# A three-stage attention and expert kernel: each step of its blocks cut into one-engine pieces, and the pieces issued in one fixed order

## The chip, the core and the metric

The kernel runs on one core of one Trainium2 chip. TensorE (PE) multiplies matrices and transposes, VectorE (DVE) and GpSimd (POOL) work element by element, ScalarE (ACT) applies exp and copies, and SyncE (SP) starts the transfers. The time is the device time of one execution in microseconds (us). Before the change the median of three runs is 252.41 us (251.99 to 254.53).

## The reference

x is (2, 11456, 128) in float32. Three layers follow one another:

```python
def mab(q, kv):                       # attention, scale = 1/sqrt(128)
    s = scale * (q @ kv.transpose(0, 2, 1))
    s = s - s.max(-1, keepdims=True)
    a = np.exp(s)
    a /= a.sum(-1, keepdims=True) + 1e-09
    return a @ kv
h = mab(I, x)                         # 32 inducing points look at all tokens of a batch
x1 = mab(x, h).reshape(22912, 128)    # every token looks at the 32 rows of h

logits = x1 @ phi                     # 32 slots, softmax over all 22912 tokens
d = np.exp(logits - logits.max(0)); d /= d.sum(0) + 1e-09
slots = (d.T @ x1).reshape(8, 4, 128) # 8 experts with 4 slots each
slot_out[e] = np.maximum(slots[e] @ w1[e], 0) @ w2[e]
c = np.exp(logits - logits.max(1)); c /= c.sum(1) + 1e-09
x2 = c @ slot_out                     # a softmax over the slots of each token

# third layer: cosine logits to 8 expert vectors, argmax, out = gate * (relu(x2 @ w1[e]) @ w2[e])
```

## The kernel before, in words

The tokens are cut into 12 blocks, six for each batch: five of 4 quads (a quad is 4 tiles of 128 tokens) and one of 2 quads. A thirteenth, "sp", holds the tokens left over. Each block goes through two phases.

**Phase 1** (lines 168 to 222) makes h of each batch. `p1_transpose` turns the tokens on PE (tile xTps) and copies them to xT, but only for the blocks in `ON_PE`; for the others xT comes ready by a transfer. `p1_scores` makes the scores s against the inducing points, their extreme mb, the running extreme mn, and on ACT e = exp and corr, the factor for what was summed before. `p1_etrans` transposes e (eTps), and `p1_h` makes the weighted sums (hps) and adds them to hacc, times corr. When the sixth block of a batch is done, `finish_h` makes hT from hacc (tiles fps, den, hT; lines 276 to 319) and from hT what phase 2 needs: BD, hst and a few bounds. A block's phase-2 scores read hT of its batch, so none can start before hT exists.

**Phase 2** (lines 321 to 459): `p2_scores` (s against hT), `p2_soft` (transposes s2T, maximum mx, difference sh, exp), `p2_a2q` (transposes a2q), `p2_logits` (lps; the row sums sm and their reciprocal; the weights a on POOL; logits lT; column maximum ml). `p2_max` and `p2_max2` keep a running maximum over the tokens: ml is transposed (mps), reduced (m32b), spread (dg, mps) and joined with the old one (mnew); cr is the factor exp(old - new); d = exp(lT - mnew). `p2_slot` multiplies a by d on PE (slps) and adds the product to acct, which POOL has multiplied by cr (lines 451 to 458). `eprep` (lines 560 to 566) makes exp of lT less its row maximum for the second softmax, and `etrans` transposes it (eTps) into ET.

**After the blocks** comes the expert layer of the slots (`slot_mlp`: tiles sips, smps, l1ps, hTps, sops), between whose steps `fill` puts some `eprep` and `etrans`; then the third layer's gate (tiles hint, gmp; `gate_pass` with gps), the load of the one expert that all tokens take and products with its weights (STps, Aps), and `out_pass` (ops, ob, the stores).

**What sets the order.** The string SEQ (line 1089) names the steps, one letter for one step of the next block; `emit` calls it, and a step issues its instructions on all its engines at once. A scheduler then places the instructions in each engine's queue, within what their data allow. SP issues a block's two loads when the scores of the fourth block before it are issued; xt has 4 buffers and xT, ET and the weights share 10 of another kind. In PSUM there are 2 wide tiles (xTps, s, lps, slps) and 4 narrow ones (fps, eTps, hps, s2, s2T, a2q, mps).

Of the kernel before, what the change touches and what calls it, by code (L numbers as in the profile page):

```python
# [1256 lines left out]
```

## Time and profile before

| | |
|---|---|
| Median of three runs | 252.41 us (251.99 to 254.53) |
| The profiled execution's own time | 253.27 us |
| Its span, first to last instruction | 251.6 us |
| Mean granted clock of PE | 0.876 of full speed |
| Busy: PE, DVE, ACT, POOL | 188.5, 164.9, 91.7, 66.2 us (75, 66, 36, 26%) |
| Moved by DMA | 41.87 MB |

The profiled execution lies 0.86 us above the median and 1.67 us above its own span. Busy time is the time in which an engine works on an instruction; PE's includes what a lower clock adds to it, so a stage can show a busy PE that is only slow. The shares differ from stage to stage, so the stages are to be read apart.

### The profile page before, as it was taken

What the parts mean: (1) busy time and instruction counts of PE and PEld (TensorE: products, weight loads), DVE (VectorE), ACT (ScalarE), POOL (GpSimd) and SP (SyncE); (2) the same over time, 40 slices, a digit from 0 to 9 for tenths busy, and PEclk for the clock granted to TensorE, in tenths of its full rate; (3) what the DMA queues carried; (4) which work ended last, traced back from release to release, by engine and by line L of the source; (5) the groups of instructions that cost most, each with busy time, mean ns of one, the idle gap of its engine ahead of it and who ended that gap; (6) DMA issues with size and microseconds to landing.
All of it is one profiled execution on the core that took longest, in us unless ns stands there. A gap on an engine that the chain in (4) does not pass through costs nothing.

```text
span 251.6 us, 4408 instructions
## 1 busy us (share of the span) xinstructions
PE 188.5 (75%) x1575; PEld 129.5 (51%) x1575; DVE 164.9 (66%) x585; ACT 91.7 (36%) x219; POOL 66.2 (26%) x75
## 2 busy tenths in 40 slices
PE   0786787689999769996869697969939795853900
PEld 0653454345576625673758525759826573532700
DVE  3366254626788985889997533254799869998440
ACT  2374543135575116564546407210122441322300
POOL 2000000001126235656465400001012762262420
PEclk9999999659999967998898779995795999997685
DMA  6996789988323895300000000031000577153491
GB/s 224 357 399 234 300 310 408 427 280 306 114 102 125 313 354 184 154 0 1 1 0 4 0 3 0 3 95 73 3 0 0 229 320 288 75 218 125 206 374 47
DMA packets 9104, 41.87 MB, mean 166 GB/s; under 512 B 1100, under 2 KB 2292, under 8 KB 5748
## 3 DMA queue, kind: packets, MB, share of 16 engines
q1 hardware_dynamic: 9076, 41.53, 43.4%
q8 instruction: 14, 0.23, 0.4%
q14 instruction: 14, 0.11, 0.2%
HBM read 29.79 MB, written 11.73 MB: 165 GB/s over the span
## 4 chain that ended last, share of the span: by engine, by line
PE 47%; DVE 32%; ACT 7%; issue 6%; DMA 3%; SPq 1%; POOL 1%; DVEq 0%; ACTq 0%
PE s L88 9%; PE ops L88 4%; PE gps L88 4%; PE eTps L85 4%; DVE ob L653 4%; PE slps L88 3%; DMA xTsp<-in_x_t 3%; PE l1ps L88 3%; PE lps L88 3%; PE hps L88 3%; DVE ml L96 2%; PE s2T L85 2%; DVE mb L96 2%; DVE lT L379 2%; DVE mx L96 2%
## 5 line engine op out<-in xcount | busy, mean ns | idle before, releaser
L88 PE MATMUL ops<-BDA,ET 64*128 64x256 f32 x180 | 29.7, 470 | 11.2 <-DVE ob L653 6.2
L384 POOL TENSOR_TENSOR a<-sh,sm 128x512 f32<-128x512 f32 (+2 forms) x13 | 12.1, 933 | 78.8 <-DVE sm L372 71.4
L88 PEld LDWEIGHTS ops<-BDA,ET 64*128 64x128 f32 x180 | 20.2, 231 | 19.1 <-DVE ob L653 9.5
L657 POOL TENSOR_TENSOR ob<-ob,scall 128x1024 f32<-128x1024 f32 x10 | 19.1, 1911 | 19.8 <-ACT ob L93 15.4
L88 PE MATMUL gps<-BDg,ET 128*128 128x164 f32 x90 | 19.9, 364 | 3.8 <-DVE BDg L755 1.9
L88 PEld LDWEIGHTS gps<-BDg,ET 128*128 128x128 f32 x90 | 15.4, 220 | 8.0 <-DVE a2q L599 3.9
L653 DVE TENSOR_TENSOR ob<-ops,scall 128x1024 f32<-128x1024 f32 x12 | 14.7, 1221 | 4.3 <-PE ops L88 4.1
L93 ACT ACTIVATE ob<-ops 128x1024 f32<-128x1024 f32 x10 | 10.2, 1022 | 19.7 <-PE ops L88 18.2
L611 POOL TENSOR_SCALAR eq<-au 128x256 f32<-128x256 f32 (+3 forms) x4 | 4.4, 1105 | 49.0 <-ACT au L93 49.0
L96 DVE TENSOR_REDUCE mb<-s 128x1 f32<-128x512 f32 (+1 forms) x12 | 7.6, 643 | 13.6 <-PE s L88 13.6
L88 PE MATMUL slps<-d,a 128*128 128x128 f32 x90 | 15.1, 311 | 0.6 <-POOL acct L454 0.6
L88 PE MATMUL s<-xT,hT 128*32 128x512 f32 (+1 forms) x96 | 15.4, 652 | 0.0
L88 PEld LDWEIGHTS slps<-d,a 128*128 128x128 f32 x90 | 13.0, 218 | 3.7 <-POOL d L423 1.7
L88 PE MATMUL s<-xT,IT 128*32 128x512 f32 (+1 forms) x96 | 14.0, 575 | 1.2 <-ACT xT L93 1.2
L88 PE MATMUL hps<-xt,eT 128*32 128x128 f32 x352 | 14.2, 288 | 0.7 <-ACT eT L93 0.7
L93 ACT ACTIVATE au<-gps 128x72 f32<-128x72 f32 (+1 forms) x23 | 5.3, 229 | 24.0 <-PE gps L88 23.9
L88 PE MATMUL lps<-BD,a2q 128*128 128x132 f32 x90 | 14.0, 297 | 0.0
L88 PEld LDWEIGHTS lps<-BD,a2q 128*128 128x128 f32 x90 | 12.0, 202 | 3.1 <-DVE dall L347 0.8
L565 POOL TENSOR_TENSOR lT<-lT,mx 128x512 f32<-128x512 f32 (+2 forms) x13 | 12.0, 929 | 5.7 <-DVE mx L96 5.6
L88 PEld LDWEIGHTS hps<-xt,eT 128*32 128x32 f32 x352 | 10.6, 115 | 5.4 <-ACT eT L93 2.9
L599 DVE TENSOR_TENSOR a2q<-gps,lT 128x256 f32<-128x256 f32 (+1 forms) x23 | 9.4, 412 | 6.2 <-ACT au L93 6.1
L193 ACT ACTIVATE eq<-s,mn 128x512 f32<-128x512 f32 (+1 forms) x12 | 7.8, 651 | 14.2 <-DVE mn L190 12.5
(284 smaller groups left out, 401.3 us busy)
## 6 DMA issues: line engine op xcount, KB each, us to landing
out<-ob SPq DMA_DIRECT2D x10, 1024.0 KB, 3.9
xt<-in_x SPq DMA_DIRECT2D x9, 1024.0 KB, 9.5
xT<-in_x_t SPq DMA_DIRECT2D x7, 1024.0 KB, 8.1
w1s<-in_moe_w SPq DMA_DIRECT2D x4, 1024.0 KB, 6.0
w2s<-in_moe_w SPq DMA_DIRECT2D x4, 1024.0 KB, 6.9
xt<-in_x SPq DMA_DIRECT2D x4, 512.0 KB, 3.7
xT<-in_x_t SPq DMA_DIRECT2D x2, 512.0 KB, 5.4
out<-ob SPq DMA_DIRECT2D x2, 512.0 KB, 5.0
```

The lines of the kernel that those rows point to most:

```text
L85: nc.tensor.matmul(dst, lhsT=src, rhs=idn, is_transpose=True, start=True, stop=True)
L88: return nc.tensor.matmul(dst, lhsT=l, rhs=r, start=start, stop=stop)
L93: S.activation(out=o, in_=i, func=AF.Copy, **kw)
L96: V.tensor_reduce(out=o, in_=i, axis=AX.X, op=op, **kw)
L193: S.activation(out=e, in_=ps[:, 0:128 * n], func=AF.Exp, scale=-1.0, bias=mn, accum_out=sb)
L379: V.tensor_tensor(out=lT[:, t0:t0 + 4 * n, :].rearrange("p (i g) s -> p i g s", g=4), in0=pv[:, :, 0:128].rearrange("p i (g s) -> p i g s" ...
L384: G.tensor_tensor(out=a2, in0=t, in1=r.unsqueeze(2).to_broadcast([128, 4 * n, 32]), op=ALU.mult)
L565: G.tensor_tensor(out=e, in0=lT[:, t0:t0 + nt, :], in1=lx.unsqueeze(2).to_broadcast([128, nt, 32]), op=ALU.subtract)
L599: V.tensor_tensor(out=q, in0=pv[:, :, E + 1:NW], in1=Eall[:, ts, :], op=ALU.mult)
L611: G.tensor_scalar(out=ge, in0=d, scalar1=0.0, scalar2=None, op0=ALU.is_ge)
L653: V.tensor_tensor(out=o.rearrange("p (i r g) c -> p i r g c", i=m, r=2), in0=pv, in1=sc.rearrange("p (i r g) -> p i r g", i=m, r=2).unsque ...
L657: G.tensor_tensor(out=o, in0=o, in1=sc.unsqueeze(2).to_broadcast([128, 4 * m, C]), op=ALU.mult)
```

## The change

Every step function becomes a generator that stops after each piece that one engine does: `p1_chain` for the twelve blocks of phase 1 (letters a to l in SEQ), `p2_chain` for phase 2 (A to M), `e_chain` for `eprep` (n to z), `grp_chain` for the running maximum (0 to 6), `h_chain` for the two batches (< and >), and one each for the left-over tokens ($) and the third layer's expert vectors (@). A letter of the new SEQ moves its chain on by one piece. `in_order` then ties each instruction of PE, DVE, ACT and POOL to the one before it on the same engine, in the order written, so that the scheduler reorders nothing there.

With it come changes to the work. Block 2 is transposed on PE too, so that its xT isn't loaded; of the copies of xT one in two goes to DVE. Blocks 0 to 7 now stand ahead of "sp" in phase 2, and the running maximum is updated for two blocks at once: 7 groups in place of 13. The slps of a group's blocks of one batch add up in one PSUM tile, so acct is multiplied and added to once for them. sm's addition, dg and some copies move from DVE to ACT; the denominator in hacc goes from DVE to POOL for 10 of 12 blocks; cr is taken from PSUM and made with two instructions on ACT; BD is one masked multiplication; the left-over tokens join h in PE's accumulation rather than in hacc. The loads of blocks 0, 1 and 2 are issued ahead of the left-over tokens' own, w1 after the last hps. `fill`'s first call makes two transposed groups of ET in place of three, and the transposes of ET that the old SEQ made ahead of the expert layer are gone from there.

```diff
-    ON_PE = (0, 1, 3)
+    ON_PE = (0, 1, 2, 3)
...
-    def p1_transpose(k, h):
+    def p1_chain(k):
...
+        for h in range((n + 1) // 2 if k in ON_PE else 0):
+            m = min(2, n - 2 * h)
+            ps = ps_w("xTps").rearrange("p (c n) -> p c n", c=2)
+            for c in range(m):
+                for t in range(4):
+                    transp(ps[:, c, 128 * t:128 * t + 128], xt_t[k][:, 8 * h + 4 * c + t, :], ident)
+            yield
+            for c in range(m):
+                (acopy if c == 0 else V.tensor_copy)(xT_t[k][:, 8 * h + 4 * c:8 * h + 4 * c + 4, :].rearrange("p a t -> p (a t)"), ps[:, c])
+            yield
         ps = ps_w("s1")
         xv4 = xT_t[k].rearrange("p (i g) t -> p i g t", g=4)
         for g in range(4):
             mm(ps[32 * g:32 * g + 32, 0:128 * n].rearrange("p (i t) -> p i t", t=128), IT, xv4[:, :, g, :])
-        mb = ty([128, 1], F32, "mb")
+        if k + 4 < NB:
+            load_block(k + 4)
+        yield
...
         mn = ty([128, 1], F32, "mn", bufs=6)
...
+        S.activation(out=corr, in_=mold, func=AF.Exp, scale=-1.0, bias=mn)
+        (V if k % NBB == NBB - 1 else G).tensor_scalar(out=hacc[b][:, C:C + 1], in0=hacc[b][:, C:C + 1], scalar1=corr, scalar2=sb, op0=ALU.mult, op1=ALU.add)
...
+        for i, c in enumerate((corr, wsp)):
+            V.tensor_scalar(out=W_h[b][:, i, :], in0=stack4[:, 0, :], scalar1=wgt, scalar2=c, op0=ALU.mult, op1=ALU.mult)
+        yield
...
+        for i, h_ in ((1, hsp), (0, hacc[b])):
+            mm(ps[:, 32:64], h_[:, C:C + 1].to_broadcast([128, 128]), W_h[b][:, i, :], i == 1, i == 0)
+        ps2 = ps_a("fps")
+        for i, h_ in ((1, hsp), (0, hacc[b])):
+            mm(ps2[:, 0:32], h_[:, 0:C], W_h[b][:, i, :], i == 1, i == 0)
+        yield
...
+        V.tensor_tensor(out=BD[b][:, 0:128].rearrange("p (g s) -> p g s", g=4), in0=ps[:, 0:32].unsqueeze(1).to_broadcast([128, 4, 32]),
+                        in1=gmask.unsqueeze(2).to_broadcast([128, 4, 32]), op=ALU.mult)
...
+            acopy(BD[B][rg, rg], ps[rg, 0:32])
...
-        V.tensor_scalar(out=r4, in0=pv[:, :, 128:132], scalar1=1e-9, scalar2=None, op0=ALU.add)
+        yield
+        acopy(r4, pv[:, :, 128:132], bias=1e-9)
+        yield
         V.reciprocal(r, r)
+        yield
+        a2 = wk([128, 4 * n, 32], F32, "a2", bufs=5)
+        G.tensor_tensor(out=a2, in0=t, in1=r.unsqueeze(2).to_broadcast([128, 4 * n, 32]), op=ALU.mult)
+        yield
...
+    def grp_chain(gi):
+
+        m = len(groups[gi])
         ps = ps_b("mps")
-        transp(ps[0:32, 0:128], ml, ident)
+        for at in range(m):
+            transp(ps[0:32, 128 * at:128 * at + 128], ml_t[gi][:, at, :], ident)
+        yield
         m32 = ty([32, 1], F32, "m32b")
-        vred(m32, ps[0:32, 0:128])
+        vred(m32, ps[0:32, 0:128 * m])
+        yield
         dg = ty([32, 32], F32, "dg")
-        V.tensor_scalar(out=dg, in0=ident[0:32, 0:32], scalar1=m32, scalar2=None, op0=ALU.mult)
-        z_t[k] = (n, a2, t0, nt, dg)
-
-    def p2_max2(k):
-        n, a2, t0, nt, dg = z_t[k]
-        ps = ps_w("mps")
-        R["mm2"] = mm(ps[:, 0:32], ones[0:32, :], dg).ins
+        acopy(dg, ident[0:32, 0:32], scale=m32)
+        yield
+        ps = ps_b("mps")
+        mm(ps[:, 0:32], ones[0:32, :], dg)
+        yield
         mold = st2["m"]
-        mnew = ty([128, 32], F32, "mnew", bufs=8)
+        mnew = ty([128, 32], F32, "mnew", bufs=5)
         V.tensor_tensor(out=mnew, in0=ps[:, 0:32], in1=mold, op=ALU.max)
         cr = ty([128, 32], F32, "cr", bufs=4)
-        V.tensor_tensor(out=cr, in0=mold, in1=mnew, op=ALU.subtract)
-        S.activation(out=cr, in_=cr, func=AF.Exp)
+        V.tensor_tensor(out=cr, in0=ps[:, 0:32], in1=mold, op=ALU.subtract)
...
+        for k in groups[gi]:
+            n, a2, t0, nt = z_t[k]
...
+            else:
+                d = wk([128, nt, 32], F32, "d")
+                eng = V if k == groups[-1][0] else G
+                eng.tensor_tensor(out=d, in0=lT[:, t0:t0 + nt, :], in1=mb, op=ALU.subtract)
+                z_t[k] = (n, a2, d, d)
+            yield
+            subbed.add(k)
+        S.activation(out=cr, in_=cr, func=AF.Relu)
+        S.activation(out=cr, in_=cr, func=AF.Exp, scale=-1.0)
+        yield
+        for k in groups[gi]:
+            n, a2, d, t = z_t[k]
+            if k == "sp":
+                for rg, c, o in SPD:
+                    S.activation(out=d[rg, o, :], in_=d[rg, o, :], func=AF.Exp)
+            else:
+                S.activation(out=d, in_=t, func=AF.Exp)
+            yield
+        yield from p2_slot(gi, cr, mnew)
+
...
+    def p2_slot(gi, cr, mnew):
+        for b in range(B + 1):
+            ks = [k for k in groups[gi] if (B if k == "sp" else blocks[k][0]) == b]
+            if not ks:
+                continue
+            ps = ps_w("slps")
+            todo = []
+            for k in ks:
+                n, a2, d, _ = z_t.pop(k)
+                todo += [(a2[:, 4 * i:4 * i + 4, :].rearrange("p t s -> p (t s)"), d[:, 4 * i:4 * i + 4, :].rearrange("p t s -> p (t s)")) for i in range(n)]
+            for i, (a_, d_) in enumerate(todo):
+                mm(ps[:, 0:128], a_, d_, i == 0, i == len(todo) - 1)
+            yield
...
+    def e_chain(k):
         t0, nt = btiles(k)
...
+    nc.sync.dma_start(out=ind_sb, in_=inducing)
     load_block(0)
-    nc.sync.dma_start(out=ind_sb, in_=inducing)
     load_block(1)
+    load_block(2)
...
-    load_block(2)
...
-    order2 = list(range(NBB)) + ["sp"] + list(range(NBB, NB))
+    order2 = list(range(NBB + 2)) + ["sp"] + list(range(NBB + 2, NB))
...
+    chains = {"abcdefghijkl"[k]: p1_chain(k) for k in range(NB)}
+    chains.update({"ABCDEFGHIJKLM"[i]: p2_chain(order2[i]) for i in range(n2)})
+    chains.update({"nopqrstuvwxyz"[i]: e_chain(ek(i)) for i in range(n2)})
+    chains.update({"0123456"[i]: grp_chain(i) for i in range(len(groups))})
+    chains.update({"<": h_chain(0), ">": h_chain(1), "$": sp_phase1(), "@": emb_setup()})
...
+    def in_order(mark):
+
+        last = {}
+        for i in nc.cur_bb.bb.instructions[mark:]:
+            if i.engine in (mybir.EngineType.PE, mybir.EngineType.DVE, mybir.EngineType.Activation, mybir.EngineType.Pool):
+                if i.engine in last:
+                    tc.add_manual_dep(i, last[i.engine].name, mybir.DependencyInfo(mybir.DependencyClass.NoSync, mybir.DependencyReason.DATA), reason="in_order")
+                last[i.engine] = i
...
+        "aaaaabaababaabbacb$@bcb$bc@$@b@cdb@cddcc$@$dcdccdedcdefd$fed$feged<e<gfge<<fg<f<gfg<gh<Ah<hB<Ah<Ah<i"
+        "ABh<AiB<hAiB<CA<BAC<BA<iBACiABCiBACDBABCDinjCBDjCBjEDC0jEk0jCo0CD0j0k0DCkEjClD0klDkEnlk0D>0lkoFDlp0l"
...
+        next(chains[c], None)
+    for c in "abcdef$<@AB0CD1EF2ghijkl>GH3IJ4KL5M6":
+        for _ in chains[c]:
+            pass
+    in_order(mark2)
...
-        for c in ("eegegeg", "egeggg", "ggg")[i]:
+        for c in ("eegeg", "egeggg", "ggg")[i]:
...
```

**PE's queue at the start of the program.** itps turns the inducing points, xTps is the transposition of tokens, s the scores of a block against IT, sps and the single sps transposition belong to the left-over tokens. Before the change:

```order
L85 MATMUL itps<-ident,ind_sb 128x32
L85 MATMUL xTps<-ident,xt 128x128 x16
L88 MATMUL sps<-xTsp,IT 32x128 x4
L85 MATMUL xTps<-ident,xt 128x128 x8
L88 MATMUL s_291<-xT,IT 32x512 x4
L85 MATMUL xTps<-ident,xt 128x128 x5
L85 MATMUL sps<-ident,eq 128x128
L85 MATMUL xTps<-ident,xt 128x128 x3
L88 MATMUL sps<-a_115,eT 32x128 x4
```

And after the change:

```order
L85 MATMUL itps<-ident,ind_sb 128x32
L85 MATMUL xTps<-ident,xt 128x128 x16
L88 MATMUL s_235<-xT,IT 32x512 x4
L85 MATMUL xTps<-ident,xt 128x128 x8
L85 MATMUL eTps<-ident,eq 128x128 x4
L85 MATMUL xTps<-ident,xt 128x128 x8
L88 MATMUL hps<-xt,eT 32x128 x16
L88 MATMUL s_299<-xT,IT 32x512 x4
```

The first scores stood behind the left-over tokens' sps and the transposes of block 1's first half; now they stand right behind block 0's sixteen transposes.

**PE's queue around hT of batch 0** (hT_0). The fps rows on whf make hT; the one on phi_sb, the transposition of hT_0 and the one on rr belong to what `finish_h` makes out of it; s rows on IT are phase 1, on hT_0 phase 2. Before the change:

```order
L88 MATMUL hps<-xt,eT 32x128 x8
L88 MATMUL fps<-whf,hacc_94 128x32 x2
L88 MATMUL fps<-phi_sb,hT_0_88 128x32
L85 MATMUL fps<-ident,hT_0_88 128x128
L88 MATMUL fps<-hT_0_88,phi_sb 32x32
L88 MATMUL s_679<-xT,IT 32x512 x4
L88 MATMUL fps<-rr_632,ones 128x96
L85 MATMUL enps<-ident,hw 128x8
L85 MATMUL eTps<-ident,eq 128x128 x4
L88 MATMUL s_672<-xT,hT_0_88 32x512 x4
```

And after the change:

```order
L88 MATMUL hps<-xt,eT 32x128 x24
L88 MATMUL fps<-whf,hsp 128x32
L88 MATMUL fps<-whf,hacc_94 128x32
L88 MATMUL fps<-whf,hsp 128x32
L88 MATMUL fps<-whf,hacc_94 128x32
L88 MATMUL s_668<-xT,IT 32x512 x4
L88 MATMUL s_681<-xT,hT_0_88 32x512 x4
L88 MATMUL fps<-phi_sb,hT_0_88 128x32
L88 MATMUL s_697<-xT,hT_0_88 32x512 x4
```

The hps of block 6 have moved ahead of hT, and behind hT two blocks' phase-2 scores now stand among the rest of `finish_h`, whose later rows were in one piece and are now spread out.

**PE's queue at the third layer's gate** (gmp). gps is `gate_pass`, STps and Aps are products with the chosen expert's weights, eTps the transposes of ET. Before the change:

```order
L88 MATMUL hint<-ien,hw 128x8
L88 MATMUL gmp<-ien,soT 128x8
L88 MATMUL gmp<-soT 128x32
L88 MATMUL gps<-BDg,ET 128x164 x6
L88 MATMUL STps<-soT,wexp 128x34 x4
L88 MATMUL gps<-BDg,ET 128x164 x2
L88 MATMUL STps<-soT,wexp 128x34 x4
L88 MATMUL gps<-BDg,ET 128x164 x6
L88 MATMUL Aps<-wexp,sh 64x128 x8
```

And after the change:

```order
L88 MATMUL hint<-ien,hw 128x8
L88 MATMUL gmp<-ien,soT 128x8
L88 MATMUL gmp<-soT 128x32
L85 MATMUL eTps<-ident,lT 128x128 x10
L88 MATMUL gps<-BDg,ET 128x164
L85 MATMUL eTps<-ident,lT 128x128
L88 MATMUL gps<-BDg,ET 128x164
L85 MATMUL eTps<-ident,lT 128x128 x8
L88 MATMUL gps<-BDg,ET 128x164
L85 MATMUL eTps<-ident,lT 128x128 x6
L88 MATMUL gps<-BDg,ET 128x164 x3
L88 MATMUL STps<-soT,wexp 128x34 x7
```

Twenty-five transposes of ET now stand behind gmp, between it and the STps, where none stood before.

## Rows read from the trace of the kernel before

**Rows 1.** Stretches: start:end, us, busy us per engine (x instructions), clock, DMA, GB/s.

```profile
0.00:43.77 43.77, 28.56 (x326) 18.43 (x326) 20.02 (x119) 19.35 (x51) 1.59 (x11) 1.00 0.85 318
43.77:78.20 34.43, 31.63 (x323) 18.53 (x323) 22.44 (x71) 16.24 (x35) 5.26 (x5) 0.85 0.66 250
78.20:141.20 63.00, 51.21 (x370) 37.29 (x371) 54.11 (x186) 29.85 (x74) 34.15 (x41) 0.89 0.28 101
141.20:165.20 24.00, 21.55 (x246) 13.05 (x247) 7.25 (x31) 7.99 (x20) 0.62 (x1) 0.86 0.01 2
165.20:189.87 24.67, 18.12 (x91) 15.90 (x90) 17.73 (x77) 4.07 (x17) 2.36 (x4) 0.78 0.13 43
189.87:251.60 61.73, 37.45 (x223) 26.31 (x223) 43.32 (x106) 14.19 (x25) 22.27 (x15) 0.83 0.48 192
```

**Rows 2.** PE's timeline: start us, us, what xcount [idle before <-releaser].

```profile
6.50 3.67 PE L85 MATMUL xTps<-ident,xt 128*128 128x128 f32 x16
...
12.03 0.78 PE L88 MATMUL sps<-xTsp,IT 128*32 128x128 f32 x8 [1.85 <-DMA xTsp<-in_x_t]
...
14.64 1.23 PE L88 MATMUL s<-xT,IT 128*32 128x512 f32 x8
...
20.44 1.06 PE L88 MATMUL hps<-xt,eT 128*32 128x128 f32 x32
...
24.21 1.10 PE L85 MATMUL xTps<-ident,xt 128*128 128x128 f32 x8
...
43.92 0.38 PE L88 MATMUL fps<-phi_sb,hT 128*128 128x32 f32 x2 [1.09 <-DVE hT L283]
...
47.41 0.71 PE L88 MATMUL fps<-rr,ones 32*128 32x96 f32 x2 [1.94 <-DVE mn L190]
...
49.11 1.94 PE L88 MATMUL s<-xT,hT 128*32 128x512 f32 x8
...
61.53 1.06 PE L88 MATMUL s<-xT,hT 128*32 128x512 f32 x8
...
77.54 0.64 PE L88 MATMUL s<-xT,IT 128*32 128x256 f32 x8
...
141.22 0.52 PE L88 MATMUL sips<-dgp,hst 128*128 128x32 f32 x2 [1.81 <-DVE dgp L484]
...
167.49 3.06 PE L88 MATMUL gps<-BDg,ET 128*128 128x164 f32 x12 [1.89 <-DVE BDg L755]
```

**Rows 3.** Groups by line and form, whole run: busy us, mean ns | idle, releaser.

```profile
L407 DVE TENSOR_TENSOR cr<-mnew 128x32 f32<-128x32 f32 x12 | 5.8, 480 | 0.0
...
L96 DVE TENSOR_REDUCE m32b<-mps 32x1 f32<-32x128 f32 x13 | 3.5, 273 | 1.1 <-PE mps L85 0.8
...
L396 DVE TENSOR_SCALAR dg<-ident,m32b 32x32 f32<-32x32 f32 x13 | 3.0, 232 | 0.0
...
L371 DVE TENSOR_SCALAR sm<-lps 128x16 f32<-128x16 f32 x10 | 1.6, 166 | 2.0 <-PE lps L88 2.0
...
L458 DVE TENSOR_TENSOR acct<-acct,slps 128x128 f32<-128x128 f32 x8 | 2.2, 277 | 4.2 <-PE slps L88 4.2
...
L522 DVE COPY hTb<-hTps 128x512 f32<-128x512 f32 x2 | 1.4, 692 | 4.4 <-PE hTps L85 4.4
...
L85 PE MATMUL eTps<-ident,lT 128*128 128x128 f32 x45 | 7.4, 300 | 1.1 <-ACT ET L93 1.1
...
L88 PE MATMUL mps<-dg,ones 32*128 32x32 f32 x26 | 5.4, 290 | 1.7 <-DVE mnew L405 0.9 <-DVE acct L458 0.8
```

**Rows 4.** Timeline near 123 us, POOL and DVE at the same time.

```profile
123.04 1.27 POOL L423 TENSOR_TENSOR d<-lT,mnew 128x512 f32<-128x512 f32 x1
...
123.24 1.12 DVE L407 TENSOR_TENSOR cr<-mnew 128x32 f32<-128x32 f32 x1
```

**Rows 5.** Line 407 alone: count, least/median/longest ns.

```profile
L407 DVE TENSOR_TENSOR cr<-mnew x12: 173/283/1121, 77.9 to 136.5; 128x32 f32<-128x32 f32 x12
```

**Rows 6.** Groups again: the transposes of ET.

```profile
L93 ACT ACTIVATE ET<-eTps 128x512 f32<-128x512 f32 x9 | 5.1, 595 | 1.5 <-PE eTps L85 1.5
```

More of the change, by code (lines that the diff above doesn't have):

```diff
@@ L215, in p1_h @@
                 mm(ps[32 * g:32 * g + 32, 0:C], eT[:, i, g, :], xt_t[k][:, 4 * i + g, :], i == 0, i == n - 1)
+        yield
         V.scalar_tensor_tensor(out=hacc[b][:, 0:C], in0=hacc[b][:, 0:C], scalar=corr, in1=ps[:, 0:C], op0=ALU.mult, op1=ALU.add)
-        V.scalar_tensor_tensor(out=hacc[b][:, C:C + 1], in0=hacc[b][:, C:C + 1], scalar=corr, in1=sb, op0=ALU.mult, op1=ALU.add)
-    xsp = wk([128, 3, C], F32, "a2", bufs=4)
+        if k == NB - 1:
+            for p in range(4):
+                load_w1(p)
+    dsp = const.tile([128, 4, 32], F32, name="dsp")
+    xsp = wk([128, 3, C], F32, "a2", bufs=5)
     xTsp = const.tile([128, 3, 128], F32, name="xTsp")
@@ L316, in attn_moe_moe_kernel @@
     z_t = {}
+    groups = []
+    group_of = {}
     R = {}
@@ L1046, in emit @@
-    def emit(c, lim):
-        nb_ = NB if c in f1 else n2
-        while ptr[c] <= min(lim, nb_ - 1):
-            k = ptr[c]
-            if c in before and ptr[before[c]] <= k:
-                return
-            if c in f1:
-                if c == "H" and k == NBB and not done_h[0]:
-                    return
-                f1[c](k)
-                if c == "S" and k + 4 < NB:
-                    load_block(k + 4)
-                if c == "S" and k == NB - 1:
-                    for p in range(4):
-                        load_w1(p)
-                if c == "S" and (k + 1) % NBB == 0:
-                    sp_all()
-                    weigh_h(k // NBB)
-            else:
-                if c == "s" and not done_h[1 if k >= NBB else 0]:
-                    return
-                if c == "w" and k >= 9:
-                    with tc.issue_after(R["mm2"]):
-                        f2[c](order2[k])
-                else:
-                    f2[c](order2[k])
-            ptr[c] += 1
-            if c == "H" and (k + 1) % NBB == 0:
-                b = k // NBB
-                finish_h(b)
-                done_h[b] = True
-                if b == 0:
-                    emb_setup()
@@ L1080, in attn_moe_moe_kernel @@
-    sp_done = []
-    def sp_all():
-        if not sp_done:
-            sp_done.append(1)
-            sp_phase1()
-            for b in range(B):
-                sp_merge(b)
-    SEQ = (
-        "TUTxSUETSHUETSHUETSHUETSHUETSHEUTSHUEsTStHUEsTaStHUElsTaStHmUElssTntaStHmUwE"
-        "lsnaaStHmEllaHmwlsntmnsweetmasslntanwwtesmlnaaweetmsllnawetmlmsnaewtmlnawemlnnwemwnwweggggg"
+        yield
+    groups += [order2[i:i + 2] for i in range(0, n2, 2)]
+    gfirst = [0]
+    for gi, ks in enumerate(groups):
+        gfirst.append(gfirst[-1] + len(ks))
+        for at, k in enumerate(ks):
+            group_of[k] = (gi, at)
@@ new lines, in ek @@
+    def ek(i):
+        return SPB if order2[i] == "sp" else order2[i]
+    chains = {"abcdefghijkl"[k]: p1_chain(k) for k in range(NB)}
[3 more added lines that the diff above has]
+    chains.update({"<": h_chain(0), ">": h_chain(1), "$": sp_phase1(), "@": emb_setup()})
+    ptr = {c: 0 for c in "eg"}
+    def emit(c, lim):
+        while ptr[c] < min(lim + 1, n2):
+            k = ek(ptr[c])
+            if c == "g":
+                if ptr["e"] <= ptr[c]:
+                    return
+                etrans(k)
+            else:
+                for _ in chains["nopqrstuvwxyz"[ptr[c]]]:
+                    pass
+            ptr[c] += 1
@@ L1092, in attn_moe_moe_kernel @@
     )
+    mark2 = len(nc.cur_bb.bb.instructions)
     for c in SEQ:
-        if c == "x":
-            sp_all()
-        else:
-            emit(c, ptr[c])
-    for c in "TUSEHstalmnw":
-        emit(c, 99)
-    assert all(ptr[c] == (NB if c in f1 else n2) for c in ptr if c not in "eg")
+        next(chains[c], None)
+    for c in "abcdef$<@AB0CD1EF2ghijkl>GH3IJ4KL5M6":
+        for _ in chains[c]:
+            pass
+    in_order(mark2)
     for p in range(4):
```

213 lines of the change are left out of this document (97 added, 116 removed).

## The prediction, made before the changed kernel ran

> **What bounds the kernel now.** I read the stretches first [rows 1]. I cut them at hT of batch 0 (43.77 us), at the last phase-1 scores (about 78.2), at the expert layer's first product sips (141.2), at the gate (165.2) and at the first output product (189.87). The reader is to compare PE's and DVE's busy time with each length. Up to 43.77, PE works 28.56 us and DVE 20.02: neither is full, and the DMA engines are busy 0.85 of the time. From there to 78.20 PE works 31.63 of 34.43, at a granted clock of 0.85. From 78.20 to 141.20 DVE works 54.11 of 63.00 (86%) and PE 51.21, at 0.89. The last three stretches are hardly touched by the change.
>
> Then PE's timeline [rows 2], to see why PE is idle in the first stretch and slow in the second. The first scores of the program start at 14.64, though block 0's transposes end at 10.17: in between PE waits 1.85 for the left-over tokens' transfer and works on sps and on eight transposes of block 1. Behind hT, PE waits 1.09 for DVE before fps at 43.92 and 1.94 at 47.41, and the next phase-2 scores take 1.94 where the same form at 61.53 takes 1.06: that is about the ratio of the clock's two levels, 1.2 and 2.4 GHz, right behind idle time.
>
> Last, the groups [rows 3] for what the running maximum costs DVE.
>
> **The change, stretch by stretch.** The sum is made against the profiled execution's 253.27, which is 0.86 above the median.
>
> *Start to hT of batch 0.* The first scores can start when the sixteen transposes (to 10.17) and a copy (0.6 [rows 6]) are done, near 11 in place of 14.64. PE gets block 2's sixteen transposes: 2.2 at 1.10 for eight [rows 2]. DVE gets eight copies of the form that takes 0.69 on line 522 [rows 3], 5.5 in all, beside 20.02 in 43.77; if they delay a score, PE waits, and that is one end below. Four eTps and sixteen hps of block 6 come ahead of hT: about 0.6 and 1.06 [rows 2], 1.7. PE's work is then 28.6 + 2.2 + 1.7 = 32.5 from 6.5 on. That ends at 39.0 without a wait; I allow 1.5 for the handovers from hacc to hT, and take 40.5: **-3.3**. Block 2's xT (1 MB of what 318 GB/s moved in 43.77, some 3.3 us) is not loaded, so the transfers allow the same. Ends: -5.0 (no wait) and 0 (the copies and the earlier hps eat it).
>
> *hT to the last phase-1 scores.* PE's 31.63 at 0.85 is 26.9 of work at full clock. 1.7 of it is done already. By the two orders some five PE steps that stood here now come after the last phase-1 scores (an slps, half-block scores, an a2q, an mps pair, an eTps; 0.5 to 0.9 each), 3.3 in all. 21.9 is left. What `finish_h` hands back and forth is now between other blocks' steps, so the waits of 1.09 and 1.94 go and a steady PE gets its clock back; I leave 2.6 for waits, nearly the 2.8 that the stretch had, since the same handovers are made in a fixed order: 24.5, **-9.9**. Ends: 21.9 (no wait), and 21.9 / 0.85 + 2.8 = 28.6.
>
> *To sips.* DVE first. cr was 5.8 in 12; now it is 7, with PSUM as an input. I take 0.18, near the least of line 407 [rows 5], 1.3 in all: -4.5. dg goes (-3.0), sm goes (-1.6), acct's sums are 3 in place of 8 at 0.28 (-1.4), m32b is 7 in place of 13, longer by half (-0.6) [rows 3]: -11.1, of which about a tenth lies ahead of 78.2, so -10. The steps handed on from the stretch before bring some 2. DVE is at 46, and at the 86% of now that is 53.5. PE: 51.21 at 0.89 is 45.6; plus 3.3, less twenty eTps that leave this stretch (0.13 each at full clock, -2.6), less six mps products (5.4 / 13 each, -2.5) [rows 3]: 43.8. At PE's present share (51.21 of 63.00) that is 53.9. The two agree, which is why I take **53.5, -9.5**, though both engines could be fuller. Ends: 46 (DVE without a gap), and 43.8 / 0.89 + 11.8 idle as now = 61.0. ACT, with dg, sm and a second cr instruction on it, has 29.85 in 63, and POOL, less five of its multiplications of acct, 34.15: neither reaches the path.
>
> The price of cr is where a row can be weighed. cr took 1.12 at 123.24 while POOL's d ran from 123.04 for 1.27 [rows 4], and its least is 0.173 [rows 5]: it ends nearly when d ends. The Trainium skill ("SBUF — State Buffer", section "SBUF: two separate sides") says that a VectorE operation with two SBUF inputs and a GpSimd operation take turns on a shared pair of ports, locked for a whole instruction. The rows agree; and as one input now comes from PSUM, by that rule the new cr would not wait. If it does all the same, seven at the mean of 0.480 [rows 3] are 3.4, and DVE saves 2.1 less.
>
> *Expert layer.* It makes five fewer transposes (7.4 / 45 each, 0.8 [rows 3]) and about one fewer copy of ET (0.6 [rows 6]): **-1.5**, with ends of -3 and 0. *Gate.* Twenty-five transposes and their copies now stand behind gmp, at 0.16 each 4.1. PE's wait of 1.89 before gps at 167.49 [rows 2] hides some ten of them; the other fifteen delay gps and STps: **+2.5**, with ends of 0 and +5. The copies' cover is ACT's idleness (4.07 busy in 24.67). Output: nothing. SP issues w1 later, behind the last hps; the DMA engines are at 0.28 between there and sips [rows 1], so I cost it at nothing, and if it weren't covered l1ps would wait for w1.
>
> The sum: -3.3 - 9.9 - 9.5 - 1.5 + 2.5 = -21.7, so 231.6 on the profiled execution, or **231** by the median.
>
> **The rivals.**
>
> *The work goes but PE is no faster.* The clock stays at 0.85 and 0.89 and the idle time stays: 28.6 and 61.0, so -5.8 and -2.0 in place of -9.9 and -9.5; with the other terms -10.1, **242**. For it: the clock was already lower in stretches where PE was 92% and 81% busy. Against it: it was at 1.00 in the first stretch, where PE was 65% busy [rows 1], and low after idle time with a chain of handovers. The Trainium skill ("TensorE: Matmul & The Clock Gate", section "What's actually happening") calls the throttled state the default, released by activity; by that a denser PE would get its clock back, as in the main case, and rows 2 agree for 49.11.
>
> *The order fills both engines.* 21.9 and 46 for the two stretches: -12.5 and -17.0, together -31.8, **221**. For it: DVE and PE have that little to do. Against it: no stretch now comes over 92% on either.
>
> *Slower: a fixed order pays for every handover.* Each engine now waits for exactly its next instruction, even where a later one is ready. PE has 129 groups in its timeline from 43.92 to 141.22 [rows 2], and is idle 2.8 + 11.8 = 14.6 in them: 0.11 each. The new order has 109 rows there. With 21.9 + 43.8 of work at the clocks of now, 75.0, and w of waiting a row, the two stretches take 75.0 + 109 w against 97.4, and the other terms give -2.3: it is even at w = 0.23. At 0.3 the sum is +8.0, **260**. Single waits of 1 to 2 us as at 47.41 would have to be common. Durations assumed wrongly in one place shift all behind it.
>
> *The change buys what isn't on the path.* w near 0.23: within 2.5 of now.
>
> **Chances.** The main case 0.56, the unfilled PE 0.22, the full engines 0.12, no change 0.04, slower 0.06. The range: 220 takes in the full engines' 221, and 244 the unfilled PE with 2 to spare for a gate at its end; the ends of the two large terms, one at a time (-2.6 and +4.1, -7.5 and +7.5 about the sum), lie within it. No change and slower, 10 in 100, and the tails of the two other rivals stay outside. A measurement of this kernel can tell about 1% (2.5 us) from no change. Faster by more: 0.56 + 0.22 + 0.12 = 0.90; same 0.04; slower 0.06.
>
> **What would show it.** First scores near 11; hT near 40.5; last phase-1 scores starting near 64.5; sips near 118.5; DVE busy about 46 between the last two; cr near 0.18; the clock above 0.9 in the second and third stretch; STps later behind gmp by 2 to 3. Wrong would be a hT later than 43, which the copies on DVE would explain; a PE wait of more than 1 us that recurs block by block; or phase 2 as long as before with a DVE of 46.

## The result and the profile after

The changed kernel takes **233.91 us** (median of four runs, 231.31 to 237.08) against 253.17 before (median of four, the three runs above among them): a ratio of **0.9204, interval 0.9098 to 0.9309**. The forecast was 231, range 220 to 244. Ratios here count only the runs within 1.5% of a kernel's fastest, so one can differ from the quotient of two medians, which is given beside it where that matters. The first profiled execution of the change took 237.08 (span 235.3), above the median, so a second one of the same kernel (234.31, span 232.7) is read beside it.

The stretches of the first, cut at the same events as [rows 1], with the third cut once more where the last phase-2 scores end:

```profile
0.00:42.30 42.30, 31.54 (x391) 20.79 (x391) 24.36 (x119) 17.61 (x46) 3.78 (x18) 1.00 0.89 343
42.30:64.68 22.38, 22.33 (x257) 13.37 (x253) 17.73 (x49) 13.96 (x36) 5.63 (x8) 1.00 0.68 266
64.68:93.61 28.93, 27.57 (x248) 17.79 (x248) 24.53 (x74) 19.14 (x56) 16.80 (x19) 0.94 0.65 254
93.61:121.44 27.83, 20.78 (x123) 17.97 (x122) 22.65 (x66) 15.17 (x44) 18.52 (x23) 0.82 0.01 1
121.44:147.32 25.88, 22.02 (x241) 14.52 (x242) 6.95 (x30) 6.41 (x14) 0.00 (x0) 0.80 0.01 1
147.32:170.50 23.18, 17.47 (x115) 14.51 (x114) 17.02 (x75) 7.68 (x25) 2.36 (x4) 0.94 0.14 46
170.50:235.30 64.80, 41.48 (x223) 28.62 (x223) 44.50 (x107) 14.23 (x25) 22.14 (x15) 0.74 0.45 183
```

And of the second (first and last stretch):

```profile
0.00:40.99 40.99, 29.50 (x391) 19.89 (x391) 24.24 (x119) 17.62 (x46) 3.78 (x18) 1.00 0.93 352
...
167.81:232.70 64.89, 41.49 (x223) 28.59 (x223) 44.45 (x107) 14.25 (x25) 22.15 (x15) 0.74 0.45 182
```

The reader is to see three regimes. From hT to the last phase-1 scores PE is busy 22.33 of 22.38 at full clock, where it had been 31.63 of 34.43 at 0.85. It stays full (27.57 of 28.93) up to the last phase-2 scores. In the 27.83 behind them no engine is: PE 75% at a clock of 0.82, DVE 81%. Before the change the last phase-2 scores ended at 121.51, and 19.69 us stood behind them:

```profile
121.51:141.20 19.69, 14.35 (x98) 12.82 (x98) 17.64 (x56) 11.55 (x28) 13.30 (x16) 0.91 0.01 2
```

So the scores are done 28 us earlier, and 8 of that is given back in a longer end of phase 2. The output stage has the work of before, and takes 3 us longer at a lower clock (0.74 for 0.83).

PE's timeline of the first execution, the rows that answer to [rows 2]:

```profile
5.26 3.67 PE L85 MATMUL xTps<-ident,xt 128*128 128x128 f32 x16 [2.32 <-DMA xt<-in_x]
10.34 1.93 PE L88 MATMUL s<-xT,IT 128*32 128x512 f32 x8 [1.41 <-DVE xT L179]
...
41.67 1.07 PE L88 MATMUL s<-xT,IT 128*32 128x512 f32 x8
42.55 1.04 PE L88 MATMUL s<-xT,hT 128*32 128x512 f32 x8
43.52 0.41 PE L88 MATMUL fps<-phi_sb,hT 128*128 128x32 f32 x2
...
51.15 0.46 PE L88 MATMUL fps<-rr,ones 32*128 32x96 f32 x2
...
64.04 0.64 PE L88 MATMUL s<-xT,IT 128*32 128x256 f32 x8
...
121.44 0.83 PE L88 MATMUL sips<-dgp,hst 128*128 128x32 f32 x6 [1.16 <-DVE dgp L480]
```

In the second execution the first scores are done faster:

```profile
9.91 1.06 PE L88 MATMUL s<-xT,IT 128*32 128x512 f32 x8 [1.42 <-DVE xT L179]
```

Between hT and fps on rr there are now 7 us of other work and no wait; before there were 1.94 of wait, and then scores at half clock.

Stages of every profile, in us (what each kernel is stands in the next section). The variants ran in three groups, and the kernel before, measured again beside each, had medians of 253.0 to 253.5; so a variant's median is compared with the changed kernel's, 233.9, directly.

| kernel | median of runs | to hT | to last ph.-1 scores | to sips | expert layer | gate | output |
|---|---|---|---|---|---|---|---|
| before | 253.2 | 43.8 | 34.4 | 63.0 | 24.0 | 24.7 | 61.7 |
| changed, first | 233.9 | 42.3 | 22.4 | 56.8 | 25.9 | 23.2 | 64.8 |
| changed, again | 233.9 | 41.0 | 22.4 | 56.2 | 25.1 | 23.2 | 64.9 |
| old order | 248.0 | 43.3 | 31.5 | 62.1 | 22.8 | 24.8 | 61.7 |
| h at once | 244.3 | 41.4 | 26.9 | 59.3 | 27.6 | 23.2 | 64.8 |
| two updates | 246.6 | 42.5 | 24.4 | 63.7 | 27.4 | 23.2 | 64.9 |
| cr from SBUF | 236.8 | 42.4 | 22.4 | 57.7 | 25.0 | 23.2 | 65.1 |
| copies on ACT | 233.7 | 40.8 | 22.4 | 55.1 | 25.1 | 23.2 | 64.9 |
| xT of block 2 loaded | 234.1 | 42.1 | 22.4 | 55.5 | 25.8 | 23.2 | 64.9 |
| unread transposes | 236.0 | 42.2 | 22.4 | 54.8 | 27.2 | 23.2 | 65.1 |
| ten behind gmp | 231.9 | 42.7 | 22.4 | 55.5 | 27.7 | 20.8 | 61.9 |
| ET in the end of phase 2 | 227.8 | 43.4 | 22.4 | 56.0 | 21.7 | 20.8 | 61.5 |
| eight groups there | 235.2 | 39.9 | 22.4 | 57.4 | 25.9 | 24.5 | 62.1 |
| five there, copies on ACT | 226.9 | 39.8 | 22.4 | 55.5 | 23.3 | 21.0 | 65.1 |

### The profile page after: what moved, and what is told of

It reads as the page before. It is cut to its first block, busy times and chain, and to the rows that moved or that the text cites. A ratio compares the mean times of both kernels' runs of the same rounds, so it can differ in the third digit from the quotient of the medians.

```text
span 235.3 us, 4376 instructions
## 1 busy us (share of the span) xinstructions
PE 183.2 (78%) x1587; PEld 127.6 (54%) x1587; DVE 157.7 (67%) x515; ACT 94.2 (40%) x244; POOL 69.2 (29%) x85
## 4 chain that ended last, share of the span: by engine, by line
PE 53%; DVE 25%; ACT 8%; issue 5%; POOL 2%; DMA 2%; SPq 0%; DVEq 0%; ACTq 0%; POOLq 0%
PE s L88 9%; PE lps L88 5%; PE gps L88 5%; PE eTps L85 4%; DVE ob L704 4%; PE slps L88 4%; PE ops L88 4%; PE xTps L85 3%; PE hps L88 3%; PE l1ps L88 3%; PE sops L88 2%; PE s2T L85 2%; PE a2q L85 2%; DVE xT L179 2%; ACT eq L197 2%
## 5 line engine op out<-in xcount | busy, mean ns | idle before, releaser
L88 PE MATMUL ops<-BDA,ET 64*128 64x256 f32 x180 | 31.2, 476 | 10.0 <-DVE ob L704 5.8
L200 POOL TENSOR_SCALAR hacc<-hacc,corr,sb 128x1 f32<-128x1 f32 x10 | 3.4, 342 | 48.9 <-ACT corr L199 45.6
L396 POOL TENSOR_TENSOR a<-sh,sm 128x512 f32<-128x512 f32 (+2 forms) x13 | 12.1, 934 | 14.7 <-DVE sm L393 10.6
L88 PE MATMUL s<-xT,IT 128*32 128x512 f32 (+1 forms) x96 | 12.8, 606 | 3.7 <-DVE xT L179 3.7
L452 POOL TENSOR_TENSOR d<-lT,mnew 128x512 f32<-128x512 f32 (+1 forms) x11 | 13.4, 1224 | 5.3 <-DVE cr L438 4.2
L88 PE MATMUL slps<-d,a 128*128 128x128 f32 x88 | 14.4, 329 | 0.5 <-ACT d L465 0.5
L88 PE MATMUL s<-xT,hT 128*32 128x512 f32 (+1 forms) x96 | 13.1, 620 | 0.0
L85 PE MATMUL xTps<-ident,xt 128*128 128x128 f32 x64 | 11.0, 332 | 2.7 <-DMA xt<-in_x 2.3
```

The lines of the kernel that those rows point to most:

```text
L85: nc.tensor.matmul(dst, lhsT=src, rhs=idn, is_transpose=True, start=True, stop=True)
L88: return nc.tensor.matmul(dst, lhsT=l, rhs=r, start=start, stop=stop)
L396: G.tensor_tensor(out=a2, in0=t, in1=r.unsqueeze(2).to_broadcast([128, 4 * n, 32]), op=ALU.mult)
L452: eng.tensor_tensor(out=d, in0=lT[:, t0:t0 + nt, :], in1=mb, op=ALU.subtract)
```

## The experiments

**The change once more.**

> The changed kernel itself, once more, so that the variants have it beside them on one chip. Expected: 231 to 235 us, ratio to the kernel before 0.91 to 0.93. Its first profile (235.3 us) had hT of batch 0 at 42.3, the last phase-1 scores ending at 64.7 and sips at 121.4, and half clock in much of what follows 100 us. If the 26.3 us of the expert layer and the 64.8 of the output stage (24.0 and 61.7 before) came from the clock of that one execution, a profile with a mean clock near 0.89 should give 24 to 25 and 61 to 62; if they came from the change, they stay.

233.86 us (227.84 to 235.06). Expert layer and output stage stay long (25.05 and 64.89), so the output stage's length isn't one execution's chance. But the six runs are at clocks of 0.876 to 0.891 for 232.8 to 235.1, and 0.930 for 227.84: the same program moves by 5 to 7 us, and the short run is the one with the higher clock.

**The old order with the new operations.**

```diff
-    for c in SEQ:
-        next(chains[c], None)
...
-    in_order(mark2)
+    for c in OLD_SEQ:
+        old_step(c, old[c])   # a step of before: S moves p1_chain on by 3, t p2_chain by 3, ...
```

> The operations of the changed kernel in the order of the old one: its SEQ drives whole steps, each of which moves its chain on by several pieces at once; the fixed order is dropped, and the expert layer makes as many transposed groups as before. Theory 1 (the order of the pieces brings most of the gain, because PE no longer waits for a chain): 242 to 248 us, and PE idle behind hT as before. Theory 2 (the gain is the removed work: 11 us on DVE, six maximum updates, one load): 233 to 238. My sum leaves about two thirds to the order, so near 243.

247.97 us, ratio 0.9812 (0.9767 to 0.9857). The removed and shifted work is worth 5 us under the old order; the order, with the place of ET's transposes that goes with it, 14. Theory 1 holds, though the order's part is larger than I had put it. In the profiles the order is worth 17 us up to sips (136.87 against 119.58), and 4 of these are lost again in the stages behind, which take 109.3 here and 113.1 in the changed kernel. The run drops the new sequence and its being fixed together; no run parts the two. Its stretch behind hT:

```profile
43.31:74.81 31.50, 29.88 (x305) 17.32 (x305) 18.08 (x50) 16.55 (x41) 5.08 (x8) 0.84 0.70 258
```

DVE has only 18.08 to do there, as in the changed kernel (17.73): the same work, with the wait and the low clock of before.

**Each batch's h in one piece.**

```diff
     for c in SEQ:
         next(chains[c], None)
+        if c in nh:              # nh counts the letters < and >
+            nh[c] += 1
+            if nh[c] >= 7:
+                for _ in chains[c]:
+                    pass
```

> One part of the order is undone: from the product that makes hT on, each batch's chain is issued in one piece, with nothing of other blocks between its steps; everything else stands as in the changed kernel. Theory 1 (the gain behind hT, 34.4 to 22.4 us, comes from laying other blocks' work between the steps of this chain): PE waits for DVE and ACT at each of the five handovers, 0.5 to 1.5 each, and its clock falls behind them; the stretch from hT to the last phase-1 scores is 4 to 8 us longer, the second batch's chain costs another 2 to 4, the time is 240 to 246. Theory 2 (the gain comes from the order of the blocks' own steps): under 2 us longer.

244.33 us, ratio 0.9650 (0.9595 to 0.9706), 10 more than the changed kernel. Theory 1. PE's timeline shows that the waits are the smaller part:

```profile
41.43 0.41 PE L88 MATMUL fps<-phi_sb,hT 128*128 128x32 f32 x2 [0.62 <-DVE hT L295]
...
43.08 0.71 PE L88 MATMUL fps<-rr,ones 32*128 32x96 f32 x2 [0.92 <-DVE rr L326]
43.72 1.94 PE L88 MATMUL s<-xT,IT 128*32 128x512 f32 x8
45.42 3.64 PE L88 MATMUL s<-xT,hT 128*32 128x512 f32 x16
```

Two waits, 1.5 us in all, and small products; then three blocks' scores take 5.3 in place of 3.2, at half clock. The stretch is 4.5 longer: PE is idle 0.97 of it in place of 0.05 (most of the first wait lies ahead of the cut at hT) and busy 25.92 in place of 22.33, at a granted clock of 0.87 in place of 1.00. The way to sips is 3 longer, as theory 1 said for the second batch, and the expert layer 2.5, at a clock of 0.75.

**Thirteen updates of the maximum.**

```diff
+        for at in range(m - 1):
+            m32 = ty([32, 1], F32, "m32b")
+            vred(m32, ps[0:32, 128 * at:128 * at + 128])
...
+            mnew = ty([128, 32], F32, "mnew", bufs=5)
+            V.tensor_tensor(out=mnew, in0=ps1[:, 0:32], in1=mold, op=ALU.max)
```

> Each group of two blocks makes its running maximum in two updates, block by block, as if there were 13 and not 7 (the first update's cr isn't used further; the values of the last one are). It adds six each of m32b, dg, the product mps, mnew and cr, some 5 us of work on three engines, and six more handovers PE-DVE-ACT-PE-DVE. Theory 1 (the end of phase 2 is a chain of handovers through the updates): each added handover of about 1.5 us after the last scores counts, the time is 4 to 8 us longer. Theory 2 (the engines' work counts, and it has room): under 2 us longer.

246.57 us, ratio 0.9653 (0.9600 to 0.9706): 12.7 longer, beyond both. The way to sips is 63.7 in place of 56.2 and the stretch before it 2 longer, for six updates with 1.7 more of DVE work to sips (48.37 against 46.66). So more is lost than the engines' added work. Each added update is issued in one piece, and the run doesn't part that from the six updates being there at all. It doesn't show what the six saved updates were worth under the old order; there all operations together were worth 5.

**cr from SBUF.**

```diff
-        V.tensor_tensor(out=cr, in0=ps[:, 0:32], in1=mold, op=ALU.subtract)
+        V.tensor_tensor(out=cr, in0=mnew, in1=mold, op=ALU.subtract)
```

> One operand is undone: cr is again new maximum less old maximum, both in SBUF; in the changed kernel it reads one of them from PSUM and takes 0.181 us each time. Theory 1 (an operation of DVE with two inputs in SBUF waits while POOL works on SBUF, as at 123 us before the change): where POOL's d starts in the same moment, cr takes up to 1.3, the mean of the seven is 0.5 or more, and what stands behind cr on DVE (reciprocals, mx) is late; the time is 0 to 3 us longer. Theory 2 (that was chance): 0.18 to 0.2 each, and the same time within 1 us.

236.75 us, ratio 0.9310 (0.9256 to 0.9364). The line alone, of this kernel and of the changed one (least/median/longest ns):

```profile
L438 DVE TENSOR_TENSOR cr<-mnew x6: 179/192/635, 74.2 to 117.1; 128x32 f32<-128x32 f32 x6
```

```profile
L438 DVE TENSOR_TENSOR cr<-mps,mnew x6: 181/181/184, 72.5 to 113.9; 128x32 f32<-128x32 f32 x6
```

One of six was held up, 0.635; the others weren't, so for cr theory 2 is nearer, and that makes 0.5 us of DVE. But DVE is busy 2.1 longer on the way to sips (48.77 for 46.66), and 1.4 of that is another operation with two inputs in SBUF, in this kernel and in the changed one:

```profile
L752 DVE TENSOR_TENSOR D<-D,dall x2: 867/911/955, 88.3 to 109.4; 128x1 f32<-128x1 f32 x2
```

```profile
L752 DVE TENSOR_TENSOR D<-D,dall x2: 178/196/214, 85.8 to 108.3; 128x1 f32<-128x1 f32 x2
```

Both of the long ones ended within 0.02 us of an operation that POOL had begun before them (POOL at 88.09 for 1.05 and at 109.06 for 1.26), as cr did in [rows 4]. So what theory 1 names is there, but falls on whichever operation meets POOL's, and the edit moved more than cr. The 2.9 between the medians isn't explained by the clock, which is in the range of the changed kernel's runs (0.877 to 0.902 against 0.871 to 0.930); how much of it these operations cost stays open. The changed kernel still has such an operation behind the groups, and there it shows; DVE and POOL of the second execution:

```profile
113.58 2.05 POOL L615 TENSOR_TENSOR lT<-lT,mx 128x512 f32<-128x512 f32 x2
...
114.04 1.64 DVE L531 TENSOR_TENSOR cr<-mnew 128x32 f32<-128x32 f32 x2
```

**Copies of xT on ACT.**

```diff
-                (acopy if c == 0 else V.tensor_copy)(xT_t[k]...
+                acopy(xT_t[k]...
```

> Only the copies of xT are undone: both halves on ACT. In the changed kernel the first scores of a block wait for DVE's copy (3.7 us in four waits before hT), and that copy begins only when ACT's has ended. Theory 1 (the two copies run one after the other, so sharing them buys nothing): the waits stay, hT within 0.5 of 42.3, the time within 1 us of the changed kernel. Theory 2 (DVE's copies are what keeps hT at 42.3 in place of 40.5): hT near 40.5, the time 1.5 to 2 us shorter. Theory 3 (ACT is needed for exp meanwhile): hT at 43 to 44, the time 1 to 2 us longer.

233.74 us, ratio 0.9238 (0.9194 to 0.9282). The time is as theory 1 said: sharing the copies buys nothing. But hT comes at 40.78, as theory 2 said, and PE waits less for xT up to there, 1.7 in place of 3.7:

```profile
PE s L88 <- ACT xT L93: 1.7, 2, 1.2
```

In the three profiles with all copies on ACT (two more follow below, whose other edits lie behind hT) hT is at 39.8 to 40.8; in the eight that share the copies, with the same work up to hT, it is at 41.0 to 43.4. So sharing them costs 1 to 2 us up to hT; the whole time, which spreads over 3 us from run to run, doesn't show it. In the changed kernel they run one after the other:

```profile
7.26 0.60 ACT L93 ACTIVATE xT<-xTps 128x512 f32<-128x512 f32 x1 [5.12 <-PE xTps L85]
7.89 0.69 DVE L179 COPY xT<-xTps 128x512 f32<-128x512 f32 x1 [1.86 <-ACT xT L93]
```

**xT of block 2 loaded.**

```diff
-    ON_PE = (0, 1, 2, 3)
+    ON_PE = (0, 1, 3)
```

> Block 2's xT is loaded again and not transposed on PE: 16 transposes and four copies fewer, 1 MB more to load ahead of hT. Theory 1 (the start is bound by PE and the copies): hT 2 us earlier, the time 1 to 2 us shorter. Theory 2 (the start is bound by the loads, the DMA engines being at 0.90 up to hT): hT up to 3 us later, the time 1 to 3 us longer.

234.12 us, ratio 0.9229 (0.9169 to 0.9289), hT at 42.07. By the time, neither theory. PE is busy 2.6 us less up to hT than in the first execution of the changed kernel (28.92 for 31.54), but only 0.6 less than in the second (29.50), where the first scores took 1.06 as here; against that one hT comes 1.1 later. The trace shows why; DVE, then PE:

```profile
16.80 0.16 DVE L1048 RECIPROCAL itau<-taub 128x1 f32<-128x1 f32 x1 [4.34 <-DMA taub<-in_moe_tau]
16.88 1.27 DVE L179 COPY xT<-xTps 128x512 f32<-128x512 f32 x2
```

```profile
18.20 2.81 PE L88 MATMUL s<-xT,IT 128*32 128x512 f32 x16 [2.27 <-DVE xT L179]
```

A reciprocal that needs a small transfer (taub) stands ahead of two copies of xT in DVE's fixed order; the transfer lands only at 16.8, and the copies and PE wait with it. In the changed kernel the same wait is 1.1 and 2.3. So the run doesn't show what less work on PE is worth by itself.

**ET's transposes in the end of phase 2.**

```diff
     for c in SEQ:
+        if c == "*":             # five places among the last letters
+            etrans(ek(ptr["g"]))
...
```

> Twenty of ET's transposes and their five copies are put back into the end of phase 2, as before the change, where the profile of the changed kernel shows PE idle 8.4 us between 64.7 and 121.4; behind gmp ten are left in place of 25. Theory 1 (the idle time at the end of phase 2 is free): the gate gets 2 to 3 us shorter, sips stays within 0.5, the time falls by 2 to 3 us. Theory 2 (the end of phase 2 is a chain of handovers through PE and ACT, and each transposition and each copy of 0.6 lies in its way): sips moves by +2 to +3 and the time stays within 1 us.

227.84 us, ratio 0.8999 (0.8957 to 0.9041). Theory 1, and more than it said. The stretches from the last phase-2 scores to the gate:

```profile
93.53:121.79 28.26, 20.68 (x142) 17.61 (x142) 21.69 (x66) 17.45 (x49) 18.57 (x23) 0.94 0.01 1
```

```profile
121.79:143.47 21.68, 18.48 (x237) 11.39 (x237) 6.77 (x30) 5.72 (x15) 0.00 (x0) 0.92 0.01 2
143.47:164.31 20.84, 15.25 (x101) 12.68 (x100) 17.19 (x76) 5.47 (x19) 2.36 (x4) 0.98 0.15 52
164.31:225.80 61.49, 37.26 (x223) 26.20 (x223) 43.48 (x107) 14.26 (x25) 22.21 (x15) 0.83 0.48 192
```

Twenty transposes more fit into the same 28.3 us, at PE's old busy time, since its clock is 0.94. Expert layer and gate together are 5.7 shorter, the output stage 3.4.

**Unread transposes there.**

```diff
+            ps = ps_b("dumps")
+            for i in range(4):
+                transp(ps[:, 128 * i:128 * i + 128], ..., ident)   # nobody reads ps
```

> The changed kernel with twenty added transposes at the end of phase 2, at the places where the other variant had ET's; nobody reads what they make, and all of ET's own transposes stay where the change put them. So PE has 20 transposes (about 3 us) more to do, and no work is moved. Theory 1 (moving ET's transposes helped by keeping PE busy, and so the clock up, at the end of phase 2 and in the expert layer): the clock there rises from 0.76 and 0.86 to about 0.92, the expert layer falls from 25.05 to 22 or 23, the output stage may fall from 64.9 to 61.5, and the time is 2 to 5 us shorter than the changed kernel, though it does more. Theory 2 (it helped because the expert layer and the gate had less to do): sips no earlier, the rest as in the changed kernel; the same time or up to 3 us longer.

236.02 us, ratio 0.9282 (0.9237 to 0.9326). The clock in the end of phase 2 rises as theory 1 said, but it isn't carried on:

```profile
92.37:119.37 27.00, 20.52 (x141) 17.62 (x142) 22.99 (x66) 15.24 (x44) 18.53 (x23) 0.93 0.01 2
```

```profile
119.37:146.56 27.19, 23.20 (x241) 15.20 (x242) 6.95 (x30) 6.39 (x14) 0.00 (x0) 0.76 0.01 1
```

So theory 1 falls: a busier PE in the end of phase 2 doesn't of itself shorten what follows. That the kernel above gains by the work it takes out of the later stages is shown for the gate alone: 20.8 to 21.0 in all three kernels with ten transposes behind gmp, 23.2 with 25. The expert layer has the same work in that kernel and in two below (15 transposes of ET), and takes 21.7, 25.9 and 23.3:

```profile
119.62:145.52 25.90, 21.06 (x236) 13.56 (x237) 6.95 (x30) 5.72 (x15) 0.00 (x0) 0.80 0.01 1
117.66:140.93 23.27, 20.07 (x236) 11.54 (x237) 6.76 (x30) 5.72 (x15) 0.00 (x0) 0.85 0.01 1
```

Its length goes with the clock (0.92, 0.80, 0.85) and with PE's waits; what sets these stays open.

**Eight groups there, copies on ACT.**

> The variant with ET's transposes in the end of phase 2, carried further: eight groups there in place of five, so that none is left behind gmp, and the copies of xT on ACT. Theory 1 (idle time on PE at the end of phase 2 is free up to its 6.6 us): the expert layer or the gate gets another 1 to 2 us shorter; 225 to 227 us. Theory 2 (the transposes now delay the chain, and their copies on ACT the exponentials): the end of phase 2 is 1 to 2 us longer, and the time 227 to 230, no better than with five.

235.16 us, ratio 0.9256 (0.9206 to 0.9305): no better than the changed kernel. The end of phase 2 isn't longer (28.59), so theory 2's reason fails. With nothing left behind gmp the gate falls back to 24.48 at 0.77, and the expert layer, with the work that took 21.7 in the kernel with five groups, is at 0.80 and takes 25.9.

**Ten behind gmp, the end of phase 2 untouched.**

```diff
-        for c in ("eegeg", "egeggg", "ggg")[i]:
+        for c in ("eegeg", "egegggegeg", "egegeg")[i]:
```

> Fifteen of the 25 transposes of ET behind gmp are moved ahead of it, into the expert layer; the end of phase 2 stays as the change left it. In the six profiles with 25 transposes behind gmp the output stage took 64.8 to 65.1 us at a clock of 0.74, in the four with none or ten 61.5 to 62.1 at 0.83, though its work is the same. Theory 1 (the 25 behind gmp are what the output stage's clock hangs on): the output stage falls to 61.5 to 62.1, the gate to about 21, the expert layer gets 2 to 3 longer, the time is 2 to 4 us shorter than the changed kernel. Theory 2 (it hangs on the end of phase 2, or on chance): the output stage stays at 64.8, the time within 1 us.

231.93 us, ratio 0.9048 (0.8975 to 0.9121; the quotient of the medians is 0.917). Theory 1 by its numbers: gate 20.84, output 61.85, expert layer 27.74, and 1.9 us less than the changed kernel. The runs of the two overlap (227.93 to 232.67, and 227.84 to 235.06).

**Five groups there, copies on ACT.**

> Five groups of ET's transposes in the end of phase 2, and the copies of xT on ACT. If the eight groups alone made the last such variant slower, this takes 226 to 229 us, with an output stage of 61.5 and an expert layer near 22. If the copies on ACT did, or if its time hangs on where the clock happens to fall, 230 to 235.

226.85 us, ratio 0.8822 (0.8759 to 0.8884). Its runs are at 222.4, 222.5 and 224.9 with clocks of 0.944, 0.939 and 0.918, and at 228.9 to 230.5 with 0.894 to 0.896; the ratio is that of the three lower ones. The quotient of the medians is 0.897, against 0.899 for five groups with shared copies: that it is faster than that kernel isn't shown. The time is that of the first expectation, the stages aren't: the expert layer took 23.27, and the output stage 65.13 with ten behind gmp, so theory 1 of the kernel before isn't a rule. What decides where the clock falls in the output stage stays open.

## Why the prediction was right

The total was right, and the mechanism of the largest term. The other terms were off by up to 4 us, in both directions, and that they partly cancel is luck. First and second execution against the forecast:

| term | forecast | measured |
|---|---|---|
| to hT | -3.3 | -1.5, -2.8 |
| to the last phase-1 scores | -9.9 | -12.1, -12.0 |
| to sips | -9.5 | -6.2, -6.8 |
| expert layer | -1.5 | +1.9, +1.1 |
| gate | +2.5 | -1.5, -1.5 |
| output | 0 | +3.1, +3.2 |
| sum | -21.7 | -16.3, -18.9 |

*To hT.* First scores at 10.34 (near 11 forecast), hT at 42.3 and 41.0 (40.5). PE waited 3.7 us in four places for DVE's copies, as this row of its waits up to hT shows:

```profile
PE s L88 <- DVE xT L179: 3.7, 4, 1.4
```

I had named them as what could eat the gain, and put them at nothing in the sum; that is the step that failed here. With all copies on ACT the waits are 1.7 and hT is at 39.8 to 40.8, about as forecast. The first execution's hT is 1.3 later than the second's, behind first scores of 1.93 in place of 1.06 (rows above).

*To the last phase-1 scores.* Right in cause, too small in size: I left 2.6 for waits in a fixed order and there were none; 21.9 of work became 22.4. The one part of the order undone brings waits and half clock back.

*To sips.* DVE's work was right (47.2 and 46.7 for 46), cr too (0.181 for 0.18). The step that failed is the share: I let both engines be as full as before throughout, DVE at 86%, and it was 83%. In fact PE is full up to the last phase-2 scores, which end 14 to 16 us sooner after the last phase-1 scores than before, and behind them stand 28 us, in place of 20, of a chain that no engine's work bounds. The chain of waits of the second execution, near its end:

```profile
112.46 0.29 DVE m32b L96
112.75 0.02 issue
112.77 0.32 ACT dg L93
113.09 0.13 ACT cr L456
113.22 0.02 issue
113.25 0.23 ACT cr L457
113.48 0.53 ACT d L465
114.01 0.04 issue
114.05 3.60 PE slps L88 x16
...
118.18 0.46 POOL acct L501
118.64 0.02 issue
118.67 0.17 DVE dgp L480
```

It goes through every engine, and its longest piece is slps at a low clock (3.60 for sixteen; 2.45 for the same sixteen in the kernel with ET's transposes there). dg and a second instruction for cr, which I costed at nothing on ACT, stand in it.

*Expert layer and gate.* Both signs were wrong: I priced transposes by their time alone. Behind gmp the 25 fill a wait and the clock there is 0.94 for 0.78, so the gate is shorter with more in it. Over fourteen profiles it takes 24.5 to 24.8 with none behind gmp, 20.8 to 21.0 with ten, 23.2 with 25: the first ten, which I had put at nothing, gain 3.8, with the clock at 0.98 for 0.78, and the other fifteen cost 2.3, near the 2.5 of my sum. The expert layer is at 0.80 and 0.86 in the two executions. In the second the clock is that of before and PE has 0.8 less to do, as forecast, but it is idle 1.9 longer (4.3 for 2.4), most of it in two waits for DVE's copies of hTps (a like wait was 0.2 before the change):

```profile
PE hTps L85 <- DVE hTb L571: 0.8, 1, 0.8
PE sops L88 <- DVE hTb L571: 0.8, 1, 0.8
```

That the transposes taken out had covered these waits is likely, but no run puts them back alone. Over all profiles the stage takes 21.7 to 27.7.

*The rivals.* PE's clock was the right worry in the wrong place: it rose where the main case said so (1.00 up to the last phase-1 scores), and was low behind 93 us (0.82). The price of a handover in a fixed order shows in two kernels (10 and 13 us longer, in the second mixed with added work), but the order laid out here mostly avoids it.
